# A float32 attention and two-layer MLP kernel on one core: the first weight unit in half blocks, another way to the low halves of the weights, merged steps on TensorE, another order search

## The chip, the core and the metric

The kernel runs on one core of one Trainium2 chip. The metric is the device time of one execution in microseconds (us). The engines are PE (TensorE, the matrix multiplier), DVE (VectorE), ACT (ScalarE), POOL (GpSimd) and SP (SyncE, which here only issues DMAs). PE's weight loads are listed apart from its matmuls, as PEld.

## The reference

```python
# attention: B=4, H=8, S=768, D=48
for t in range(S):
    state = alpha[:, :, t, :, None] * state + np.einsum('bhd,bhe->bhde', k[:, :, t], v[:, :, t])
    y[:, :, t] = np.einsum('bhd,bhde->bhe', q[:, :, t], state)
x = y.transpose(0, 2, 1, 3).reshape(B * S, H * D)     # 3072 tokens x 384
x = ((x @ w_a) * (x @ w_b)) @ w_out                   # first MLP, 1536 wide
h = x @ w_in                                          # second MLP, 2048 wide
g = np.maximum(h, 0.0) + alpha2 * np.minimum(h, 0.0)
out = g @ w_out2
```

The weights come as float64; everything else is float32. The output has float32 accuracy.

## The kernel before

**Three products for one.** PE's fast full-width type is fp32r, which holds fewer bits than float32. So each large operand is kept as a high part, rounded to fp32r, and a low part that holds the rest, and each product is the sum of high x high, low x high and high x low (`mm3`, lines 818, 819 and 821). A large matmul is 128 x 128 weights by 512 tokens.

**Blocks, chunks, units.** The 3072 tokens are six blocks of 512, and each block is four chunks of 128. The weights of the first MLP are six units u of 256 hidden columns; a unit has three parts, a, b (up) and o (down). One step of the first MLP is one half unit with one block: an up product `pa` (9 matmuls), an up product `pb` (9), their product on DVE (line 948), its split into `gh` (ACT, 841) and `gl` (DVE, 845), and a down product into `acc` (9). The order of these steps is the list `SEGMENTS`: block 0 with units 0 and 1, block 1 with units 0 and 1, block 0 with units 2 and 3, and so on; from block 2 on a block meets all six units. The up products keep this order. The second MLP (96 steps of 18 large matmuls) follows.

**A chunk of the attention.** The recurrence is done by chunks. On DVE: two scans and a reciprocal over alpha (523, 529, 533) and a product that scales q and k (538). On PE: the transposes of the keys (`pe_k`, 606; "keys" below), the scores (553 in block 0, 563 after), then `pe_cross` (685 and 707) and `pe_own` (685 and 692) from block 1 on. Between them DVE masks the scores (626) and adds the states (712 `mid`, 715 `kept`), ACT copies the keys out (610), and ACT and DVE split the output into the high and low part of x (770, 774). In block 1 six DMAs for each chunk (line 792) then move rows of x between partitions; the up products of that block wait for them. From block 2 on `pe_own` also computes the scores of the next chunk of the same block (`ahead`, for c < 3); the keys of each chunk are a step by themselves, and the scores of a block's first chunk too.

**A weight part.** A float64 part lies as pairs of 32-bit words. ACT takes the magnitude (368); DVE makes the sign, the float32 value, its power of two and the remainder (371, 376, 380, 385); ACT rounds to the high part (391); DVE subtracts it and adds the remainder (394, 397: the low part). For the parts a, b and o of unit 0 the last two operations are matmuls on PE (422 to 424) and a copy on ACT (427); a and b of unit 0 are also done in two halves. The parts of the second MLP take the same way later and go through HBM.

**The order.** Every operation on PE, DVE, ACT and SP is an `Op` of a `Graph` with a duration, a latency and a due time (`key`). `place` makes an order for each engine from estimated times; `search` shuffles the keys (400 tries) of operations that start early, and keeps what its cost likes; `run` emits the instructions in that order. On the chip each engine follows its own list and waits at semaphores. Where the plan has a long pause on PE before block 2, `fill` puts in small matmuls that nobody reads (`wp`, line 307), as many as `(t1 - t0) * 0.7 // 110`. The matmuls of one chunk step are a `burst` on PE.

Of the kernel before, what the change touches and what calls it, by code (L numbers as in the profile page):

```python
# [14 lines left out]
F32R = mybir.dt.float32r  # L15
I64 = mybir.dt.int64
# [6 lines left out]
P = 128  # L23
CH = 128
# [8 lines left out]
LAG = 2  # L33

# [3 lines left out]
MM = 230  # L38
# [8 lines left out]
SOON = 150000  # L47
TRIES, WORLDS = 400, 2
# [13 lines left out]
class Graph:  # L62
# [27 lines left out]
    def tables(self):  # L90
        n = len(self.ops)
        self.eng = [o.eng for o in self.ops]
        self.users = [[u.n for u in o.users] for o in self.ops]
        self.soft = [[u.n for u in o.soft] for o in self.ops]
        self.hold = [[u.n for u in o.hold] for o in self.ops]
        self.before = [[] for _ in range(n)]
        for i in range(n):
            for u in self.users[i]:
                self.before[u].append((i, True))
            for u in self.soft[i]:  # L100
                self.before[u].append((i, False))

    def place(self, keys=None, order=None, dur=None, lat=None):
# [5 lines left out]
        start, end, seq, gaps, logs = [0] * n, [None] * n, [], [], {}  # L109
        free = dict.fromkeys(eng, 0)  # L110
        able = {e: [i for i in range(n) if eng[i] == e and not need[i]] for e in free}
        burst = False

        def room(p):
            log = logs.setdefault(p, [])
# [3 lines left out]
        def when(i):  # L119
            t = room(ops[i].pool) if ops[i].pool else 0  # L120
            return None if t is None else max(ready[i], t)

        for k in range(n):
            if order is None:
                best = None
                for e, l in able.items():
                    l = [(t, i) for i in l if (t := when(i)) is not None]
                    if l:
                        t = max(free[e], min(l)[0])
                        if best is None or t < best[0]:  # L130
                            best = (t, l)
                if best is None:
                    return None
                t, l = best
                i = min((i for x, i in l if x <= t), key=lambda i: (keys[i], i))
                able[eng[i]].remove(i)
            else:
                i = order[k]
                t = when(i)
                if t is None:  # L140
                    return None
                t = max(free[eng[i]], t)
# [9 lines left out]
            if o.pool:  # L152
                logs.setdefault(o.pool, []).append(self.hold[i])
            start[i], free[e], end[i] = t, t + d, t + d + lat[i]
            seq.append(i)
            for u in self.users[i]:
                ready[u] = max(ready[u], end[i] + (HOP if eng[u] != e else 60))
            if order is None:
                for u in self.users[i] + self.soft[i]:
                    need[u] -= 1  # L160
                    if not need[u]:
                        able[eng[u]].append(u)
# [34 lines left out]
    def search(self):  # L197


        rnd, ops, n = random.Random(1), self.ops, len(self.ops)  # L200
        pe = [i for i in range(n) if self.eng[i] == "PE"]
        worlds = []
        for _ in range(WORLDS):
            worlds.append(([int(o.dur * rnd.uniform(1, 1.08)) + rnd.randrange(40) for o in ops],
                           [o.lat + (rnd.randrange(1200) if o.eng == "SP" else rnd.randrange(60)) for o in ops]))

        def cost(plan):
            if plan is None:
                return float("inf")
            plans = [plan] + [self.place(order=plan[2], dur=d, lat=l) for d, l in worlds]  # L210
            if None in plans:
                return float("inf")
            ends = [max(p[1][i] for i in pe) for p in plans]
            return ends[0] + sum(ends[1:]) / max(1, len(worlds))

        keys = [float(o.key) for o in ops]
        plan = self.place(keys)
        assert plan is not None, "the operations wait for each other"
        best = cost(plan)
        late = self.latest(*plan[:3])  # L220
        first = [i for i in range(n) if plan[0][i] < SOON]
        for k in range(TRIES):
            new = late if k == 0 else list(keys)
            if k:
                mid, width, step = rnd.uniform(0, SOON), rnd.choice((3000, 10000, 30000)), rnd.choice((2500, 8000, 24000))
                for i in first:
                    if abs(plan[0][i] - mid) < width and rnd.random() < 0.5:
                        new[i] += rnd.gauss(0, step)
            other = self.place(new)
            if other is None or max(other[1][i] for i in pe) > max(plan[1][i] for i in pe) + 1000:  # L230
                continue
            c = cost(other)
            if c <= best:
                best, keys, plan = c, new, other
        return plan
# [29 lines left out]
def body(tc, akq, v, vg, w_a, w_b, w_o1, w_in, w_o2, beta, out):  # L265
# [13 lines left out]
    with ExitStack() as ctx:  # L279
# [46 lines left out]
        flat = [(n, i, s) for s, (n, u0, u1) in enumerate(SEGMENTS) for i in range(2 * u0, 2 * u1)]  # L326
        at = [T_MOE + int(k * 27 * MM * STRETCH) for k in range(len(flat) + LAG + 1)]
        due, block_at = {}, {}
        for k, (n, i, s) in enumerate(flat):
# [8 lines left out]
        def conv(src, tag, name, key, wait, sink, early=15000, on_pe=False, halves=None):  # L338
# [11 lines left out]
            ld = G.add("SP", 2100, load, key - early, wait, 4000)  # L350
            free = cring.take()
            last, highs = [], []
            for n in range(2 if halves else 1):
# [29 lines left out]
                def rest(c2=c2, word=word):  # L383
                    o = c2()
# [3 lines left out]
                def high(n=n, c1=c1, hi=hi):  # L388
                    if n == 0:
# [10 lines left out]
                d = lambda t: t // N + 40  # L400
                m = G.add("ACT", d(910), magnitude, key, [ld, *(free if n == 0 else ())], after=last, line="c1")
                x = G.add("DVE", d(550), sign, key, [m])
                x = G.add("DVE", d(930), main, key, [x])
                x = G.add("DVE", d(550), power, key, [x])
# [736 lines left out]
```

## Time and profile before

| | |
|---|---|
| median of 3 runs | 957.52 us (957.03 to 957.98) |
| the profiled execution | 956.25 us, of which 954.5 us are the span from its first to its last instruction |
| PE busy | 943.4 us (99% of the span), 6630 matmuls |
| DVE busy | 601.9 us (63%) |
| ACT busy | 254.6 us (27%) |
| granted TensorE clock | 0.998 of 2.4 GHz over the span |
| DMA | 104.48 MB, mean 109 GB/s |

The profile shows one execution. Starts are recorded; the ends of matmuls are modelled, and neighbours overlap in the records, so a matmul's cost is read from the distance of starts and not from its duration. "Idle before" an instruction is counted from the end of the one in front of it on its engine.

### The profile page before, as it was taken

Reading aid. Unit: us, or ns where it says so; the run is one execution under the profiler, and the core shown is the slowest. Engines: PE = TensorE matmul, PEld = TensorE weight load, DVE = VectorE, ACT = ScalarE, POOL = GpSimd, SP = SyncE. Lnnn points to the kernel's source line nnn. Section 1 sums busy time; section 2 is a strip of 40 time slices with the busy share of each in tenths; the row PEclk is TensorE's granted clock in tenths of the full one; section 3 lists DMA queues with packets and bytes.
Section 4 is the critical chain, followed back from the end, with each engine's and each line's share of the span. In section 5 each row is a group of like instructions: output and inputs, shape, how many; then the busy total and the mean of one; then the engine's idle time right before and its main releaser. Section 6 shows DMA issues by size and latency. Waiting matters only on the chain.

```text
span 954.5 us, 15479 instructions
## 1 busy us (share of the span) xinstructions
PE 943.4 (99%) x6630; PEld 766.0 (80%) x6630; DVE 601.9 (63%) x883; ACT 254.6 (27%) x414; POOL 2.2 (0%) x11
## 2 busy tenths in 40 slices
PE   9989999999999999999999999999999999999998
PEld 7668888878778888888888888888888888888886
DVE  8999999576788789863232255555555545545554
ACT  2445443233333433332221211121111211111211
POOL 0000000000000000000000000000000000000000
PEclk9999999999999999999999999999999999999999
DMA  9955000244455556451164540110100200200000
GB/s 340 369 199 189 16 1 10 70 138 168 154 186 197 206 211 203 180 190 67 27 240 169 186 190 1 56 45 0 67 34 1 100 1 1 100 1 1 33 1 34
DMA packets 32228, 104.48 MB, mean 109 GB/s; under 512 B 3872, under 2 KB 5408, under 8 KB 32160
## 3 DMA queue, kind: packets, MB, share of 16 engines
q1 hardware_dynamic: 32016, 103.37, 30.7%
q8 instruction: 52, 0.85, 0.4%
q14 instruction: 16, 0.13, 0.0%
q10 hardware_dynamic: 144, 0.13, 0.0%
HBM read 74.78 MB, written 26.74 MB: 106 GB/s over the span
## 4 chain that ended last, share of the span: by engine, by line
PE 95%; DVE 4%; issue 0%; ACT 0%; POOL 0%; ACTq 0%; DVEq 0%; POOLq 0%
PE acc L821 12%; PE acc L818 12%; PE acc L819 12%; PE pi L818 7%; PE pi L819 7%; PE pi L821 7%; PE pa L818 5%; PE pb L818 5%; PE pa L819 5%; PE pa L821 5%; PE pb L819 5%; PE pb L821 5%; PE both L685 2%; PE both L563 1%; PE both L692 1%; PE wp L307 1%
## 5 line engine op out<-in xcount | busy, mean ns | idle before, releaser
L841 ACT CAST gh<-ng 128x512 fp32r<-128x512 f32 x96 | 59.6, 621 | 318.9 <-DVE ng L1054 256.4
L1050 DVE TENSOR_SCALAR ng<-pi,betaT 128x512 f32<-128x512 f32 x96 | 72.1, 751 | 106.1 <-PE pi L821 105.7
L845 DVE TENSOR_TENSOR gl<-ng,gh 128x512 fp32r<-128x512 f32 x96 | 66.3, 690 | 78.3 <-ACT gh L841 78.3
L821 PE MATMUL acc<-gl,v 128*128 128x512 f32 x288 | 113.5, 394 | 0.0
L819 PE MATMUL acc<-gh,v 128*128 128x512 f32 x288 | 112.9, 392 | 0.0
L818 PE MATMUL pi<-x,v 128*128 128x512 f32 x288 | 112.8, 392 | 0.0
L819 PE MATMUL pi<-x,v 128*128 128x512 f32 x288 | 112.7, 391 | 0.0
L818 PE MATMUL acc<-gh,v 128*128 128x512 f32 x288 | 111.8, 388 | 0.0
L948 DVE TENSOR_TENSOR a_sb<-a_sb,pb 128x512 f32<-128x512 f32 x72 | 49.4, 685 | 93.6 <-PE pb L821 93.1
L818 PE MATMUL pa<-x,wa 128*128 128x512 f32 x216 | 87.3, 404 | 0.0
L818 PE MATMUL pb<-x,wb 128*128 128x512 f32 x216 | 86.4, 400 | 0.0
L818 PE MATMUL acc<-gh,wo 128*128 128x512 f32 x216 | 86.1, 398 | 0.0
L819 PE MATMUL pa<-x,wa 128*128 128x512 f32 x216 | 85.1, 394 | 0.0
L821 PE MATMUL acc<-gl,wo 128*128 128x512 f32 x216 | 85.0, 394 | 0.0
L819 PE MATMUL pb<-x,wb 128*128 128x512 f32 x216 | 84.6, 391 | 0.0
L819 PE MATMUL acc<-gh,wo 128*128 128x512 f32 x216 | 84.5, 391 | 0.0
L821 PE MATMUL pi<-x,v 128*128 128x512 f32 x288 | 81.5, 391 | 0.0
L945 ACT COPY a_sb<-pa 128x512 f32<-128x512 f32 x72 | 42.2, 586 | 135.0 <-PE pa L821 134.9
L841 ACT CAST gh<-a_sb 128x512 fp32r<-128x512 f32 x72 | 44.7, 621 | 117.8 <-DVE a_sb L948 102.3
L1054 DVE SCALAR_TENSOR_TENSOR ng<-pi,ng 128x512 f32<-128x512 f32 x96 | 66.3, 691 | 3.0
L819 PEld LDWEIGHTS acc<-gh,v 128*128 128x128 f32 x288 | 54.0, 188 | 12.6
L818 PEld LDWEIGHTS pi<-x,v 128*128 128x128 f32 x288 | 54.1, 188 | 12.2 <-DVE ng L1054 0.4
(118 smaller groups left out, 1410.5 us busy)
## 6 DMA issues: line engine op xcount, KB each, us to landing
kq<-in_akq SPq DMA_DIRECT2D x24, 512.0 KB, 4.5
w2d<-ws SPq DMA_DIRECT2D x16, 768.0 KB, 3.5
v<-w2d SPq DMA_DIRECT2D x16, 768.0 KB, 5.4
x2d<-x SPq DMA_DIRECT2D x18, 512.0 KB, 3.4
x<-x2d SPq DMA_DIRECT2D x6, 1536.0 KB, 6.9
ra<-in_akq SPq DMA_DIRECT2D x24, 258.5 KB, 4.1
v<-in_v SPq DMA_DIRECT2D x24, 256.0 KB, 5.0
rs<-in_w_in SPq DMA_DIRECT2D x8, 768.0 KB, 4.6
```

The costliest lines, as they stand in the source:

```text
L307: nc.tensor.matmul(wp, warm[:, 0:P], warm, start=True, stop=True)
L563: nc.tensor.matmul(a[hs, i, j, :], kT()[ps, j, hs], qT()[ps, j, hs], start=True, stop=True, skip_group_check=True)
L685: nc.tensor.matmul(y_of(k, half(p), part_of(h)), s["v"][part_of(h), 2 * j + i, :], s["As"][part_of(h), i, j, :], start=first, stop=False, ...
L818: nc.tensor.matmul(o, lh, rh, start=first and n == 0, stop=False)
L819: nc.tensor.matmul(o, ll, rh, start=False, stop=False)
L821: nc.tensor.matmul(o, lh, rl, start=False, stop=last and n == len(pairs) - 1)
L841: nc.scalar.copy(gq[idx][0], src())
L845: nc.vector.tensor_tensor(out=gl, in0=src(), in1=gh.bitcast(F32), op=ALU.subtract)
L945: nc.scalar.copy(b["a"], ba["t"])
L948: nc.vector.tensor_tensor(out=b["a"], in0=b["a"], in1=bb["t"], op=ALU.mult)
L1050: nc.vector.tensor_scalar(out=b["n"], in0=bh["t"], scalar1=0.0, scalar2=betaT[:, i : i + 1], op0=ALU.min, op1=ALU.mult)
L1054: nc.vector.scalar_tensor_tensor(out=b["n"], in0=bh["t"], scalar=0.0, in1=b["n"], op0=ALU.max, op1=ALU.add)
```

## The change

Six edits:

1. **Half blocks.** `SPLIT` names unit 0 with block 0. Its two steps of 512 tokens become four of 256: tokens 0 to 255 with both half units, then 256 to 511. The first two need x of chunks 0 and 1 alone.
2. **Low parts.** For all parts but those of unit 0: the low word and the low bits of the high word are put together into one signed 32-bit number (`top`, in place in the raw words; `below`), ACT makes the high part with a scale (`rounded`), and the low part is that number times the power of two of the value (`exponent`, `low`). On DVE: 371, 376, `top`, `below`, `exponent`, `low` instead of 371, 376, 380, 385, 394, 397.
3. **Low parts on PE.** For a and b of unit 0 the remainder is written as fp32r, and the third matmul is fp32r instead of float32.
4. **Merged steps.** From block 1 on keys and scores are one step (`both_of`: scores, then transposes). From block 2 on `pe_own` of each chunk is followed by scores and keys of the next chunk (`ahead["both"]`), across the end of a block too. That step now waits also for the next chunk's scaled q and k and for the bank of the transposes.
5. **Search.** Another walk: it starts from the latest start times, accepts some worse plans, 500 tries, only operations that start in the first 120 us; two other random "worlds" with less scatter; `place` keeps heaps.
6. **Estimates.** The first load is put at 1000 + 2400 ns instead of 3200 + 1500, a load of weights at 2000 + 3500 instead of 2100 + 4000, a large matmul at 229 ns instead of 230, and others by 10 to 30 ns.

```diff
+SPLIT = ((0, 0),)
-MM = 230
+MM = 229
-SOON = 150000
-TRIES, WORLDS = 400, 2
+SOON = 120000
+SEED, TRIES, WORLDS = 6, 500, 2
...
+        plan = self.place([o.key for o in ops])
+        keys = self.latest(*plan[:3])
+        plan = self.place(keys) or plan
+        best = now = (cost(plan), keys, plan)
+        rnd = random.Random(SEED)
         for k in range(TRIES):
+            new, begin = list(now[1]), now[2][0]
+            width, share = rnd.choice(((1500, 0.6), (1500, 0.6), (5000, 0.3), (15000, 0.12), (50000, 0.04)))
+            mid, step = rnd.uniform(0, SOON), rnd.choice((2000, 7000, 25000))
+            for i in range(n):
+                if begin[i] < SOON and abs(begin[i] - mid) < width and rnd.random() < share:
+                    new[i] += rnd.gauss(0, step)
+            plan = self.place(new)
+            if plan is None or last(plan) > last(now[2]) + 1000:
                 continue
+            c = cost(plan)
+            if c <= now[0] or rnd.random() < math.exp((now[0] - c) / (100 * (1 - k / TRIES) + 1)):
+                now = c, new, plan
+                best = min(best, now, key=lambda x: x[0])
...
-        flat = [(n, i, s) for s, (n, u0, u1) in enumerate(SEGMENTS) for i in range(2 * u0, 2 * u1)]
+        whole, parts = slice(0, MB), (slice(0, MB // 2), slice(MB // 2, MB))
+        flat = [(n, 2 * u + o, s, t) for s, (n, u0, u1) in enumerate(SEGMENTS) for u in range(u0, u1)
+                for t in (parts if (n, u) in SPLIT else (whole,)) for o in range(2)]
+        span = lambda t: MM if t == whole else MM // 2 + 10
+        size = lambda t, ns: ns if t == whole else ns // 2 + 80
...
-                def sub(c1=c1, hi=hi):
-                    nc.vector.tensor_tensor(out=c1(), in0=c1(), in1=hi().bitcast(F32), op=ALU.subtract)
+                def top(word=word):
+                    nc.vector.tensor_scalar(out=word(1, U32), in0=word(1, U32), scalar1=23, scalar2=None,
+                                            op0=ALU.logical_shift_left)
+                def below(c2=c2, word=word):
+                    nc.vector.scalar_tensor_tensor(out=c2().bitcast(U32), in0=word(0, U32), scalar=9,
+                                                   in1=word(1, U32), op0=ALU.logical_shift_right,
+                                                   op1=ALU.bitwise_or)
+                def rounded(n=n, c1=c1, hi=hi):
+                    b["r"] = wpool.tile([P, 2 * UC], F32R, name=f"w{name}", tag=tag)
+                    nc.scalar.mul(hi(), c1(), 1.0 + 2.0**-22)
+                def exponent(c1=c1):
+                    x = c1().bitcast(U32)
+                    nc.vector.tensor_scalar(out=x, in0=x, scalar1=0xFF800000, scalar2=None, op0=ALU.bitwise_and)
                 def low(c1=c1, c2=c2, lo=lo):
-                    nc.vector.tensor_tensor(out=lo(), in0=c1(), in1=c2(), op=ALU.add)
+                    nc.vector.scalar_tensor_tensor(out=lo(), in0=c2().bitcast(I32), scalar=2.0**-43,
+                                                   in1=c1(), op0=ALU.mult, op1=ALU.mult)
                     sink(b["r"])
...
-                        nc.tensor.matmul(o, ident, cut(c2()), start=False, stop=True)
+                        nc.tensor.matmul(o, *((plus, cut(lo())) if halves else (ident, cut(c2()))),
+                                         start=False, stop=True)
...
-            la = A("SP", 3200 if g == 0 else 720, load_a, rwait, 14000, 1500 if g == 0 else 3000, line="ra")
+            la = A("SP", 1000 if g == 0 else 720, load_a, rwait, 14000, 2400 if g == 0 else 3000, line="ra")
...
+            def keys():
+                s["kps"] = (s["kbank"] if start else att)("kps")
+                for j in range(NJ):
+                    nc.tensor.transpose(s["kps"][:, j, :], kT()[:, j, :], ident)
+            def both_of():
+                scores()
+                keys()
...
-            ahead = st[g + 1] if n > 1 and c < BC - 1 else None
+            ahead = st[g + 1] if n > 1 and g + 1 < NG else None
...
+            elif "front" in s:
+                x = pa = s["front"]
+                khold = s["khold"]
+            else:
+                x = pa = A("PE", 1150, s["both"], [k1, *aring.take(), *afree, *yfree])
+                khold = aring.last()
...
                     if ahead:
-                        ahead["scores"]()
+                        ahead["both"]()
...
+                if ahead:
+                    py = A("PE", 1900, pe_own, [z1, z2, ahead["k1"], *aring.take()])
+                    ahead.update(front=py, khold=aring.last())
+                    ahead["lhold"].append(py)
-                py = A("PE", 1460 if ahead else 900, pe_own, [z1, *([z2, ahead["k1"]] if ahead else ())])
...
+            xs = xdone[n] if t == whole else xdone[n][t.start // CH : t.stop // CH]
+            pa, ma, ba = up(at[k], [done["a", u][o], *xs], x, ("a", u), o, [up_before], t)
+            pb, mb, bb = up(at[k] + 9 * span(t), [done["b", u][o], *xs], x, ("b", u), o, [pa], t)
```

## Rows read from the trace of the kernel before

**Rows 1.** Stretches: length, then busy us (instructions) by engine, PE clock, DMA share, GB/s.

```profile
9.60:67.40 57.80, 51.72 (x801) 39.80 (x800) 55.92 (x93) 23.58 (x48) 0.00 (x0) 0.99 0.88 328
66.30:69.70 3.40, 3.34 (x38) 2.78 (x39) 3.40 (x6) 1.86 (x4) 0.00 (x0) 0.51 0.43 154
110.00:550.00 440.00, 440.00 (x3755) 356.83 (x3754) 289.21 (x425) 141.29 (x224) 0.00 (x0) 1.00 0.42 143
```

**Rows 2.** Timeline of PE, 66 to 69 us: start, us, instruction, idle before it.

```profile
66.36 1.14 PE L563 MATMUL both<-kq 48*64 48x64 f32 x32 [1.77 <-DVE x L774]
67.42 0.79 PE L818 MATMUL pa<-x,wa 128*128 128x512 f32 x1
```

**Rows 3.** Timeline of DVE, 10 to 76 us.

```profile
10.82 0.69 DVE L622 TENSOR_TENSOR As<-A,mask 128x512 f32<-128x512 f32 x1 [0.50 <-PE A L553]
...
64.75 0.95 DVE L397 TENSOR_TENSOR wa<-c,c 128x768 fp32r<-128x768 f32 x1
...
69.15 0.55 DVE L371 TENSOR_SCALAR c<-ro 128x768 uint32<-128x768 uint32 x1
...
75.42 0.69 DVE L774 TENSOR_TENSOR x<-both,x 128x512 fp32r<-128x512 f32 x1
```

**Rows 4.** Timeline of SP's DMA queue, 75 to 92 us.

```profile
76.14 4.68 SPq L792 DMA_DIRECT2D x<-x  x6
```

**Rows 5.** Timeline of PE, 84 to 89 us.

```profile
86.45 0.85 PE L821 MATMUL pa<-x,wa 128*128 128x512 f32 x3
...
88.51 0.85 PE L821 MATMUL pb<-x,wb 128*128 128x512 f32 x3
```

**Rows 6.** Timeline of PE, 163 to 166 us, around own with scores.

```profile
163.73 0.40 PE L821 MATMUL acc<-gl,wo 128*128 128x512 f32 x1
...
165.70 0.39 PE L819 MATMUL pa<-x,wa 128*128 128x512 f32 x1
```

**Rows 7.** Timeline of PE, 195 to 199 us, around own, scores and keys.

```profile
195.66 0.85 PE L821 MATMUL pa<-x,wa 128*128 128x512 f32 x3
...
198.47 0.39 PE L819 MATMUL pb<-x,wb 128*128 128x512 f32 x1
```

**Rows 8.** Timeline of PE, 236 to 239 us, around keys alone.

```profile
236.74 0.85 PE L821 MATMUL pb<-x,wb 128*128 128x512 f32 x3
...
238.10 0.40 PE L819 MATMUL acc<-gh,wo 128*128 128x512 f32 x1
```

**Rows 9.** Timeline of PE, around own alone, then around keys with scores.

```profile
285.27 0.85 PE L821 MATMUL pa<-x,wa 128*128 128x512 f32 x3
...
287.23 0.40 PE L819 MATMUL pb<-x,wb 128*128 128x512 f32 x1
...
323.40 0.85 PE L821 MATMUL pb<-x,wb 128*128 128x512 f32 x3
...
325.58 0.40 PE L819 MATMUL pa<-x,wa 128*128 128x512 f32 x1
```

**Rows 10.** Groups by line and shape: count, busy us, mean ns, idle us before.

```profile
L371 DVE TENSOR_SCALAR c<-ro 128x768 uint32<-128x768 uint32 x6 | 3.3, 551 | 0.0
L397 DVE TENSOR_TENSOR wa<-c,c 128x768 fp32r<-128x768 f32 x5 | 4.8, 950 | 0.0
L424 PE MATMUL cl<-c,plus 128*128 128x384 f32 x12 | 4.8, 485 | 0.0
L819 PEld LDWEIGHTS pa<-x,wa 128*128 128x128 f32 x216 | 41.0, 190 | 8.3
L948 DVE TENSOR_TENSOR a_sb<-a_sb,pb 128x512 f32<-128x512 f32 x72 | 49.4, 685 | 93.6 <-PE pb L821 93.1
L774 DVE TENSOR_TENSOR x<-both,x 128x256 fp32r<-128x256 f32 x4 | 1.6, 408 | 0.0
```

**Rows 11.** DMA issues: count, KB each, median us to landing.

```profile
x<-x SPq DMA_DIRECT2D x24, 64.0 KB, 3.2
ra<-in_w_a SPq DMA_DIRECT2D x6, 768.0 KB, 7.5
```

More of the change, by code (lines that the diff above doesn't have):

```diff
@@ L108, in place @@
         need, ready = [len(b) for b in self.before], [0] * n
-        start, end, seq, gaps, logs = [0] * n, [None] * n, [], [], {}
+        start, end, seq, gaps, logs = [0] * n, [None] * n, [], [], {p: [] for p in self.pools}
         free = dict.fromkeys(eng, 0)
-        able = {e: [i for i in range(n) if eng[i] == e and not need[i]] for e in free}
+        later, able = {e: [] for e in free}, {e: [] for e in free}
+        pooled = []
         burst = False
         def room(p):
-            log = logs.setdefault(p, [])
+            log = logs[p]
@@ L136, in place @@
-                able[eng[i]].remove(i)
+                t = None
+                for x in free:
+                    l, a, f = later[x], able[x], free[x]
+                    while l and l[0][0] <= f:
+                        i = heapq.heappop(l)[1]
+                        heapq.heappush(a, (keys[i], i))
+                    at = f if a else l[0][0] if l else None
+                    if x == "PE":
+                        pools = [(max(f, ready[i], b), keys[i], i) for i in pooled
+                                 if (b := room(ops[i].pool)) is not None]
+                        at = min([at] * (at is not None) + [q[0] for q in pools], default=None)
+                    if at is not None and (t is None or at < t):
+                        t, e = at, x
@@ L207, in cost @@
         def cost(plan):
[L208 to L217, printed above, removed]
+            plans = [self.place(order=plan[2], dur=d, lat=l) for d, l in worlds]
@@ L218, in search @@
+            return float("inf") if None in plans else (last(plan) + sum(map(last, plans)) / len(plans)) / 2
+        plan = self.place([o.key for o in ops])
         assert plan is not None, "the operations wait for each other"
-        best = cost(plan)
-        late = self.latest(*plan[:3])
-        first = [i for i in range(n) if plan[0][i] < SOON]
+        keys = self.latest(*plan[:3])
+        plan = self.place(keys) or plan
+        best = now = (cost(plan), keys, plan)
+        rnd = random.Random(SEED)
@@ L222, in search @@
         for k in range(TRIES):
[L223 to L230, printed above, removed]
-                continue
@@ L232, in search @@
[L232 to L235, printed above, removed]
+            new, begin = list(now[1]), now[2][0]
+            width, share = rnd.choice(((1500, 0.6), (1500, 0.6), (5000, 0.3), (15000, 0.12), (50000, 0.04)))
+            mid, step = rnd.uniform(0, SOON), rnd.choice((2000, 7000, 25000))
+            for i in range(n):
+                if begin[i] < SOON and abs(begin[i] - mid) < width and rnd.random() < share:
+                    new[i] += rnd.gauss(0, step)
@@ L413, in conv @@
                     continue
+                x = G.add("DVE", d(550), power, key, [x])
+                x = G.add("DVE", d(950), rest, key, [x])
+                x = G.add("ACT", d(840), high, key, [x], after=highs)
+                highs = [x]
                 ev = None
@@ L845, in lo, with down @@
                 nc.vector.tensor_tensor(out=gl, in0=src(), in1=gh.bitcast(F32), op=ALU.subtract)
-            h = G.add("ACT", 620, hi, key, [*deps, *gring.take()], line="gh")
-            return G.add("DVE", 700, lo, key, [h])
-        def down(idx, key, deps, hold, acc, w, o, first, last):
+            h = G.add("ACT", size(t, 620), hi, key, [*deps, *gring.take()], line="gh")
+            return G.add("DVE", size(t, 680), lo, key, [h])
+        def down(idx, key, deps, hold, acc, w, o, first, last, t=whole):
             def f():
```

206 lines of the change are left out of this document (110 added, 96 removed).

## Prediction

> **What bounds the kernel now.** I read the table of stretches first. From 110 to 550 us PE is busy in all 440.0 us while DVE works 289 of them; from 9.6 to 67.4 us PE is busy in 51.7 of 57.8 us and DVE in 55.9 [rows 1]. So there are two stages. In the late one the time is the sum of PE's steps: nine large matmuls lie between the two starts of [rows 5], 88.51 - 86.45 = 2.06 us, 0.229 us each, and nothing but shorter or fewer steps on PE can help. In the head DVE is the bound: PE's idle time there is 57.80 - 51.72 = 6.1 us, and some of its busy time is fill.
>
> Next the timelines, to find which DVE instruction ends PE's waiting for good. The longest wait ends at 66.36, behind a DVE split [rows 2]; the first up product of unit 1 starts at 67.42 [rows 2], after the low part of that weight (64.75 + 0.95 = 65.70, [rows 3]). The waiting has a second price: from 66.3 to 69.7 us the granted clock is 0.51, the 1.2 GHz level [rows 1]. At full clock this work of 3.4 us takes about half, so 1.6 us went there.
>
> There is a second date close behind. Block 1 starts when x of chunk 7 has been moved: its low part at 75.42 [rows 3], six DMAs issued from 76.14 for 4.68 us [rows 4], the last landing some 3.2 us later [rows 11], at 84.0. Block 1's first up product starts six matmuls before 86.45, at 85.08 [rows 5]. So the head can move by 1.1 us before chunk 7 too must come earlier.
>
> **Merged steps.** The price of a chunk step on PE is the distance from the last large matmul before it to the second one behind it, less the 2 x 0.229 us that these two would take (a row "x3" starts two matmuls earlier). Own with scores: 165.70 - 163.73 - 0.46 = 1.51 [rows 6]. Keys alone: 238.10 - 236.74 - 0.92 = 0.44 [rows 8]. Own, scores and keys in one, which the old order once happened to make: 198.47 - 195.66 - 0.92 = 1.89 [rows 7]. So a chunk that goes from 1.95 to 1.89 saves 0.06: 12 chunks in blocks 2 to 5, one of which had it, 0.7 us. Where a block begins the gain is larger: own alone 287.23 - 285.27 - 0.92 = 1.04, keys with scores 325.58 - 323.40 - 0.92 = 1.26 [rows 9], together 2.30 against 1.89, 0.41 each for blocks 3, 4 and 5: 1.2 us. Block 1's four steps lie in the head, and I count nothing for them. Sum: **-1.9 us** in a stage where PE never idles. What the merge costs is a longer list of things to wait for: own of a block's last chunk now also waits for the next block's scaled keys, and PE's whole queue stands behind it. The cover is DVE's slack, 151 of 440 us [rows 1]; without it one late chunk costs what DVE needs for it, a few us.
>
> **Low parts.** Removed per part are 0.55 (380) + 0.95 (385) + 0.95 (394) + 0.95 (397) = 3.40 us of DVE; added are `top`, `below`, `exponent`, `low`. The two with two tensors are like line 397, 0.95; the two with one tensor and a constant are like line 371, which reads every second word in 0.55 [rows 10]. That is 3.00, so -0.40 a part. `top` also writes every second word, which no row shows: it is between 0.55 and 0.95, and I take 0.55 for its likeness to 371; the other end makes the edit worth nothing. Before the date of 67.42 parts a and b of unit 1 count: **-0.8 us**. Later parts lie where PE is the bound, and count nothing.
>
> The Trainium skill (VectorE: DVE Perf Modes, "Mode 2×_2P — use both read ports for one tensor") lets an operation with a single tensor in SBUF run at two float32 results a cycle and names no condition on the step; by it `top` is 0.55 and the sum stays; by the slow row it would lose 0.8.
>
> **Half blocks.** On DVE the product and the split of a step are 685 ns each, and an operation on 256 columns 408 [rows 10]: 2 x 408 - 685 = 0.13, for two operations of two steps **+0.5 us**. On PE 108 matmuls of 256 columns replace 54 of 512. Free would be 0.1145 each; the other end is the record of a weight load, 0.190 [rows 10], so 0 to +8.2 us. I take +1, nearer to the free end, since at 0.229 the loads hide with nearly as much work behind them; it falls where PE has 6.1 us of idle time, so nothing of it reaches the end. In return block 0 can meet its first weights with two chunks done instead of four.
>
> A rule speaks against this edit: the Trainium skill (TensorE: Matmul & The Clock Gate, "LDWEIGHTS (loading the stationary operand)") puts a load at its columns over 1.2 GHz, 107 ns for 128 of them, however few columns then stream; by it the half matmul is just covered, by the record it would be bound by its load.
>
> **Third matmul of a and b.** Four float32 products leave, at most 4.8 / 6 = 0.8 us each [rows 10], so 0 to -3.2 us of PE work before 54 us. PE waits for DVE later in the head, so this only lengthens that wait: 0.
>
> **Estimates and fill.** The first score matmuls come late enough that DVE waits 0.50 for them at 10.82 [rows 3]; with the first load put at 3.4 us instead of 4.7 the plan's first pause, and with it the fill, is about 1.3 us shorter. **-0.5 us** of DVE time. It cancels the +0.5 of the half blocks.
>
> **Order.** How much can another order give? DVE's list before chunk 7's split at 75.42 holds work that nothing needs so soon: four operations of o of unit 1 from 69.15 [rows 3] (0.55 + 0.95 + 0.55 + 0.95 = 3.0) and three of unit 2's a (0.55 + 0.95 + 0.55 = 2.05), 5 us. Between 0 and -5 I take **-1.0**, as the chains from PE to ACT to DVE must fit between. With it and the -0.8 the wait before 66.36 (1.77 and another before it) breaks up enough that the clock stays up: **-1.6**, or 0 if it does not.
>
> **Sum.** -1.9 - 0.8 + 0.5 - 0.5 - 1.0 - 1.6 = -5.3 us. The profiled execution took 956.25 (span 954.5 and 1.75 around it), and would take 950.9; the median of the runs is 957.52, so 952.2 is what I predict for the median. A measurement can tell about 0.2%, 1.9 us: faster is below 955.6, slower above 959.4.
>
> **Rivals.**
> 1. *The second date holds.* If chunk 7 does not move, the head gives only the 1.1 us between 84.0 and 85.08: 957.5 - 1.9 - 1.1 = 954.5. For it: its chain goes through PE, ACT and six DMAs, which no edit shortens. Against it: the 5 us of work that can be put behind it.
> 2. *The order finds most of the slack.* -1.9 - 0.8 - 1.6 - 5 = 948.2. Against it: DVE would have to do everything in the best order with no gap.
> 3. *The head gives nothing*, since `top` is slow, the half blocks' DVE work eats the rest, and the clock falls in some other wait: 957.5 - 1.9 = 955.6, or up to 957.5 if the merged steps wait as much as they save. That is the case where the change does not do what it says.
> 4. *Slower: loads land late under a tighter plan.* DVE follows its list in order. The new plan reckons 5.5 us for a load of weights (before 6.1); the rows say 7.5 [rows 11], with the DMA engines at 0.88 over the head [rows 1]. Each load that is 2.0 us late for its first operation stops the scans and splits behind it by as much, and a clock drop adds 1.6. It turns slower from 7.2 us of such stalls on; three late loads and one drop, 7.6, give 957.5 - 5.3 + 7.6 = 959.8. Against it: the old plan was wrong by 1.4 too, and DVE was still busy in 55.9 of 57.8 us [rows 1].
>
> **How the numbers follow.** Forecast 0.55 (its own range 949.5 to 953.7), second date 0.18, most of the slack 0.10, nothing from the head 0.10, slower 0.07. The range that leaves out 2 in 10 reaches from the order's bound, 948.5, into the third rival, 956.0. Faster: 0.55 + 0.18 + 0.10 = 0.83; the third rival is the same, 0.10; slower 0.07.
>
> **What would show it.** In the new profile: `pe_own` steps of 1.89 us from block 2 on, no separate transposes after it, and PE still busy in all of 110 to 540 us; `top` at 0.55; starts of the half matmuls some 0.12 us apart; the first up product of unit 1 and that of block 1 both some 3 us before 67.42 and 85.08; no stretch at 0.51 of the clock after the first fill. I am wrong if block 1's first up product is not earlier, if DVE shows waits for DMA in the head, or if PE waits in the late stage.

## The result, and the profile after

The changed kernel takes 949.23 us (median of 4 runs, 948.92 to 949.48) against 957.39 (957.03 to 957.98) for the kernel before: 0.9914 of it [0.9897, 0.9931], 8.2 us faster. The profiled execution took 949.33 with a span of 947.6; 6.9 us of span are gone against the profiled 954.5 of before. The other 1.2 or so lie in the kernel before, whose runs lie above its profiled one (956.28 to 957.62 over thirteen later runs, mean granted clock 0.996 to 0.998); with the change the four runs show a clock of 1.000. The clock alone doesn't explain the 1.2: of those thirteen runs the ten at 0.998 spread from 956.28 to 957.57.

**Stretches after**, in the columns of [rows 1]: first the three stretches shown there, then 9.6 us to chunk 7's split and to block 1's first up product, and three slices of 25 us from 75 us on.

```profile
9.60:67.40 57.80, 55.48 (x906) 45.06 (x904) 57.52 (x103) 26.39 (x55) 0.00 (x0) 1.00 0.90 339
66.30:69.70 3.40, 3.40 (x108) 2.94 (x107) 3.40 (x8) 1.18 (x2) 0.00 (x0) 1.00 0.25 68
110.00:550.00 440.00, 440.00 (x3733) 358.29 (x3733) 275.56 (x422) 140.38 (x220) 0.00 (x0) 1.00 0.43 148
...
9.60:71.44 61.84, 59.52 (x971) 48.53 (x970) 61.56 (x110) 28.33 (x58) 0.00 (x0) 1.00 0.87 327
9.60:78.85 69.25, 66.93 (x1007) 54.78 (x1006) 68.97 (x122) 32.41 (x64) 0.00 (x0) 1.00 0.85 318
...
75.00:100.00 25.00, 25.00 (x111) 20.51 (x110) 25.00 (x39) 12.67 (x18) 0.00 (x0) 1.00 0.25 88
100.00:125.00 25.00, 25.00 (x185) 20.24 (x184) 25.00 (x41) 12.59 (x19) 0.00 (x0) 1.00 0.04 11
125.00:150.00 25.00, 25.00 (x187) 20.50 (x186) 24.99 (x38) 11.76 (x17) 0.00 (x0) 1.00 0.15 43
```

**The same two dates and slices of the kernel before.**

```profile
9.60:75.42 65.82, 59.74 (x918) 46.02 (x918) 63.80 (x106) 26.35 (x53) 0.00 (x0) 0.97 0.83 307
9.60:85.08 75.48, 69.40 (x961) 53.91 (x960) 73.45 (x122) 32.26 (x61) 0.00 (x0) 0.98 0.81 302
...
75.00:100.00 25.00, 25.00 (x111) 20.51 (x110) 24.13 (x36) 13.94 (x21) 0.00 (x0) 1.00 0.39 146
100.00:125.00 25.00, 25.00 (x111) 20.52 (x110) 24.66 (x36) 10.78 (x18) 0.00 (x0) 1.00 0.04 12
125.00:150.00 25.00, 25.00 (x188) 20.29 (x187) 23.36 (x36) 10.54 (x16) 0.00 (x0) 1.00 0.01 1
```

Up to chunk 7's split, DVE's idle time fell from 65.82 - 63.80 = 2.02 us to 0.28, and its busy time from 63.80 to 61.56. Up to block 1, PE's idle time fell from 6.08 to 2.32 us, and its busy time by 2.5 us, in which the stretch at 0.51 of the clock [rows 1] lies. In the slices from 75 to 150 us DVE has no gap left, and PE has none either.

**The waits of PE after**, engine, line and what it waited for: us in total, times, longest. All three rows of the answer:

```profile
PE both L624 <- DVE x L843: 1.7, 3, 1.0
PE wp L338 <- POOL ones L340: 1.4, 1, 1.4
PE kps L630 <- issue: 0.4, 1, 0.4
```

The 1.77 behind the split [rows 2] is now at most 1.0.

**Timeline of PE after**: the half matmuls, the first up product of unit 1 (60.63), PE's last wait before block 1 (63.22), block 1's first up product (78.85), and one merged step.

```profile
28.85 0.28 PE L888 MATMUL pa<-x,wa 128*128 128x256 f32 x1
28.97 0.28 PE L887 MATMUL pa<-x,wa 128*128 128x256 f32 x1
...
29.44 0.51 PE L890 MATMUL pa<-x,wa 128*128 128x256 f32 x3
...
60.63 0.51 PE L887 MATMUL pa<-x,wa 128*128 128x512 f32 x1
...
63.22 0.69 PE L624 MATMUL both<-kq 48*64 48x64 f32 x32 [0.23 <-DVE x L843]
...
78.85 0.39 PE L887 MATMUL pa<-x,wa 128*128 128x512 f32 x1
...
189.35 0.85 PE L890 MATMUL pa<-x,wa 128*128 128x512 f32 x3
190.13 0.46 PE L749 MATMUL both<-As,v 64*64 64x64 f32 x16
...
190.86 0.65 PE L624 MATMUL both<-kq 48*64 48x64 f32 x32
191.44 0.66 PE L630 MATMUL kps<-plus,kq 128*128 128x128 f32 x4
...
192.16 0.39 PE L888 MATMUL pb<-x,wb 128*128 128x512 f32 x1
```

Unit 1 starts 6.8 us earlier than the 67.42 of [rows 2], block 1 6.2 us earlier than the 85.08 worked out from [rows 5]. The merged step costs 192.16 - 189.35 - 0.92 = 1.89 us, as [rows 7].

**From PE's last wait to block 1**, before and then after, in the columns of [rows 1]. PE has no gap in either.

```profile
66.36:85.08 18.72, 18.72 (x192) 15.05 (x192) 18.57 (x31) 9.42 (x15) 0.00 (x0) 0.91 0.62 228
...
63.22:78.85 15.63, 15.63 (x195) 13.13 (x196) 15.63 (x28) 7.91 (x12) 0.00 (x0) 1.00 0.67 236
```

**Timeline of DVE after**, where [rows 3] stood: the first scores, the low part of unit 1's first weight, chunk 7's split.

```profile
11.31 0.69 DVE L691 TENSOR_TENSOR As<-A,mask 128x512 f32<-128x512 f32 x1 [0.28 <-PE A L614]
...
59.42 0.95 DVE L452 SCALAR_TENSOR_TENSOR wa<-c,c 128x768 fp32r<-128x768 int32 x1
...
71.44 0.68 DVE L843 TENSOR_TENSOR x<-both,x 128x512 fp32r<-128x512 f32 x1
```

**SP's DMA queue after**, beside [rows 4]:

```profile
72.15 3.77 SPq L861 DMA_DIRECT2D x<-x  x6
```

**The last of the six DMAs in the kernel before**, and the times from an issue to its landing of all six:

```profile
80.22 0.59 SPq L792 DMA_DIRECT2D x<-x  x1
...
DMA to landing us min/median/max: 1.8/3.9/5.1
```

**Groups by line and shape after**, beside [rows 10]: `top`, and a product of half width.

```profile
L433 DVE TENSOR_SCALAR ra<-ra 128x768 uint32<-128x768 uint32 x5 | 2.8, 557 | 0.0
L1018 DVE TENSOR_TENSOR a_sb<-a_sb,pb 128x256 f32<-128x256 f32 x4 | 1.6, 405 | 0.0
```

**Where the 6.9 us of span come from.** Block 1 starts 6.23 us earlier. Behind that point the chunk steps cost 47.49 us in sum instead of 49.33, each priced as in the prediction: -1.84. That makes -8.07, and 1.24 are given back in the second MLP, as follows; 0.1 us stays unassigned.

**Timeline of PE after, at the end of a block of the second MLP.**

```profile
621.10 0.39 PE L887 MATMUL pi<-x,v 128*128 128x512 f32 x1
...
622.47 0.85 PE L890 MATMUL pi<-x,v 128*128 128x512 f32 x3
623.30 0.51 PE L887 MATMUL pi<-x,v 128*128 128x512 f32 x1
623.65 0.40 PE L888 MATMUL pi<-x,v 128*128 128x512 f32 x1
```

**Timeline of DVE after, at the same place.**

```profile
621.30 0.75 DVE L1120 TENSOR_SCALAR ng<-pi,betaT 128x512 f32<-128x512 f32 x1 [0.58 <-PE pi L890]
621.97 0.68 DVE L915 TENSOR_TENSOR gl<-ng,gh 128x512 fp32r<-128x512 f32 x1
622.57 0.68 DVE L1124 SCALAR_TENSOR_TENSOR ng<-pi,ng 128x512 f32<-128x512 f32 x1
```

The table of PE's waits has no row for this, and PE counts as busy throughout, since the modelled end of one matmul covers the gap. It shows in the distance of starts, and in the table of waits of the weight loads (PEld), here after and then before: six waits instead of one.

```profile
PEld pi L887 <- DVE ng L1124: 2.5, 6, 0.4
...
PEld pi L818 <- DVE ng L1054: 0.4, 1, 0.4
```

In starts it reads like this. The group of nine that starts at 621.10 has its ninth matmul at 622.47 + 2 x 0.229 = 622.93. From there to the second matmul of the next group, 623.65, two steps of 0.229 would take 0.46, and took 0.72: 0.26 lost. That next group starts 0.05 us after DVE's line 1124 has read the bank `pi` (622.57 + 0.68 = 623.25). DVE is not short of time there: it stood idle for 0.58 us just before 621.30. But between its two readings of that bank (lines 1120 and 1124) it makes the split of the product before (line 915), so the bank comes free 623.25 - 621.30 = 1.95 us after the first reading began. With two banks PE needs it again after one up product in the other bank, 2.06 us, and the passing from PE to DVE and back doesn't fit into the rest. Five such ends (622.9, 689.1, 755.3, 821.5, 887.7) are new, 1.24 us in all; the one at 556.8 has its like in the kernel before, at 565.

### The profile page after: what moved, and what is told of

It is laid out like the page before. It is cut to its first block, busy times and chain, and to the rows that moved or that the text cites. A ratio compares the mean times of both kernels' runs of the same rounds, so it can differ in the third digit from the quotient of the medians.

```text
span 947.6 us, 15534 instructions
## 1 busy us (share of the span) xinstructions
PE 940.3 (99%) x6671; PEld 766.1 (81%) x6671; DVE 587.2 (62%) x887; ACT 256.1 (27%) x418; POOL 2.2 (0%) x11
## 4 chain that ended last, share of the span: by engine, by line
PE 94%; DVE 5%; issue 1%; POOL 0%; ACT 0%; DVEq 0%; ACTq 0%; POOLq 0%
PE acc L887 12%; PE acc L888 12%; PE acc L890 12%; PE pi L887 7%; PE pi L888 7%; PE pi L890 7%; PE pb L887 5%; PE pa L887 5%; PE pb L890 5%; PE pb L888 5%; PE pa L890 5%; PE pa L888 5%; PE both L749 1%; PE kps L630 1%; PE wp L338 1%; PE both L624 1%
## 5 line engine op out<-in xcount | busy, mean ns | idle before, releaser
L1018 DVE TENSOR_TENSOR a_sb<-a_sb,pb 128x512 f32<-128x512 f32 (+1 forms) x74 | 49.5, 669 | 100.6 <-PE pb L890 99.6
L887 PE MATMUL pa<-x,wa 128*128 128x512 f32 (+1 forms) x222 | 87.1, 394 | 0.0
L887 PE MATMUL acc<-gh,wo 128*128 128x512 f32 (+1 forms) x222 | 86.6, 390 | 0.0
L887 PE MATMUL pb<-x,wb 128*128 128x512 f32 (+1 forms) x222 | 86.5, 391 | 0.0
L890 PE MATMUL acc<-gl,wo 128*128 128x512 f32 (+1 forms) x222 | 85.9, 387 | 0.0
L888 PE MATMUL acc<-gh,wo 128*128 128x512 f32 (+1 forms) x222 | 85.3, 384 | 0.0
L888 PE MATMUL pa<-x,wa 128*128 128x512 f32 (+1 forms) x222 | 85.2, 385 | 0.0
L888 PE MATMUL pb<-x,wb 128*128 128x512 f32 (+1 forms) x222 | 85.2, 385 | 0.0
L911 ACT CAST gh<-a_sb 128x512 fp32r<-128x512 f32 (+1 forms) x74 | 45.2, 610 | 140.2 <-DVE a_sb L1018 129.1
L1015 ACT COPY a_sb<-pa 128x512 f32<-128x512 f32 (+1 forms) x74 | 42.6, 576 | 118.7 <-PE pa L890 118.4
L1124 DVE SCALAR_TENSOR_TENSOR ng<-pi,ng 128x512 f32<-128x512 f32 x96 | 66.3, 691 | 3.0
```

The costliest lines, as they stand in the source:

```text
L887: nc.tensor.matmul(o, lh, rh, start=first and n == 0, stop=False)
L888: nc.tensor.matmul(o, ll, rh, start=False, stop=False)
L890: nc.tensor.matmul(o, lh, rl, start=False, stop=last and n == len(pairs) - 1)
L911: nc.scalar.copy(gq[idx][0], src())
L1015: nc.scalar.copy(b["a"], ba["t"])
L1018: nc.vector.tensor_tensor(out=b["a"], in0=b["a"], in1=bb["t"], op=ALU.mult)
```

## The experiments

The theory I began with was the prediction's: DVE's list in the head is the bound, some edits shorten it, and a better order takes more. Its rivals were that the new search alone does it, and that the edits alone do. In each group all kernels were timed against the kernel before on one chip; it took 957.33, 956.89 and 957.37 us (medians) in the three groups, so raw medians of different groups can be compared to about 0.5 us. "After" is the changed kernel, 949.23.

### First group: search, seed and one estimate

**The new edits with the old search.**

```diff
-SOON = 120000
-SEED, TRIES, WORLDS = 6, 500, 2
+SOON = 150000
+TRIES, WORLDS = 400, 2
```

The body of `search` is that of the kernel before, too.

> The changed kernel with the old search (400 tries from the first plan, the old random worlds, 150 us). In the changed kernel the first up product of block 1 came 6.2 us earlier (85.08 to 78.85) and the merged steps took 1.8 us off the late stage. Theory 'order' (the new search found most of the 6.2): the head falls back by 3 us or more, 952 to 956. Theory 'edits' (half blocks, low parts and the shorter third matmul give any search this room): within 1.5 us of the changed kernel, 949 to 951.

951.26 us, 0.9940 [0.9925, 0.9955]. Block 1's first up product starts at 80.44. So 6.1 of the 8.2 us are there with the old search; the new one adds 2.0 with seed 6, and 0.4 with seed 1 (950.89, below).

**The old edits with the new search.**

```diff
-SOON = 150000
-TRIES, WORLDS = 400, 2
+SOON = 120000
+SEED, TRIES, WORLDS = 6, 500, 2
```

The lines are against the kernel before, which gets `place` and `search` of the changed one and nothing else.

> The kernel before with nothing but the new search. Theory 'order': 4 us or more of the 6.2 come with the search alone, 951.5 to 953.5. Theory 'edits': the old graph has no room, 955.5 to 957.5.

957.38 us, 1.0002 [0.9993, 1.0011]. Block 1 starts at 85.72 and unit 1 at 67.60, both a little later than before, and the clock still falls (its stretch, in the columns of [rows 1]):

```profile
66.30:69.70 3.40, 2.81 (x37) 2.31 (x38) 3.40 (x6) 1.87 (x3) 0.00 (x0) 0.66 0.79 307
```

That rules out the search, with this seed, as a cause by itself: on the old edits it found nothing.

**Another seed.**

```diff
-SEED, TRIES, WORLDS = 6, 500, 2
+SEED, TRIES, WORLDS = 1, 500, 2
```

> The changed kernel with seed 1 in place of 6: how far the order alone moves the time. Theory 'order': 1 to 3 us off, 949 to 952. Theory 'edits': the same within 0.7 us.

950.89 us, 0.9936 [0.9921, 0.9951]; block 1 at 78.43, 0.4 us earlier than with seed 6, and yet 1.7 us slower at the end. The date misleads here: nine large matmuls of a down product, 9 x 0.229 = 2.06 us, stand behind block 1's first up product with this seed and in front of it with seed 6 (9 and 18 matmuls of 512 tokens write `acc` before that date). Counted alike, block 1 would come at 80.5, 1.6 later, which is nearly all of the 1.7. Two seeds differ by 1.7 us, so a single search is no ruler for an edit of this size.

**The estimate of the second MLP's stores.** The five new stalls at the ends of blocks are also there with the old search and with seed 1 (six waits of PEld for line 1124 each), and not in the old edits with the new search (one), so the new edits or estimates bring them. The plan puts the eviction of an output tile late because it reckons its store at 1400 + 2000 ns. This run changes that one line.

```diff
-                    ring.use(G.add("ACT" if h else "SP", 1400, store, key - URGENT, [x], 2000))
+                    ring.use(G.add("ACT" if h else "SP", 700, store, key - URGENT, [x], 1300))
```

> The changed kernel with one estimate changed, that of the output stores of the second MLP (700 + 1300 ns in place of 1400 + 2000). Up to 550 us all orders stay as they were; at the five block borders of the second MLP three up products stand in a row in place of four. In the changed kernel each of these borders shows a pair of starts on PE 0.25 us late. Theory: DVE needs 0.75 + 0.69 + 0.69 = 2.13 us for each up product in a row and PE 2.06, so the fourth waits for its bank; with three in a row 1.2 us come back, 948.0. Rival: the waiting moves to the down products behind them, 949.2.

947.78 us, 0.9902 [0.9886, 0.9919]: 1.45 faster than after, at the same start of block 1 (78.75), with the same order up to 550 us. PE at the same end of a block:

```profile
622.39 0.85 PE L890 MATMUL pi<-x,v 128*128 128x512 f32 x3
623.08 0.39 PE L887 MATMUL acc<-gh,v 128*128 128x512 f32 x1
623.31 0.39 PE L888 MATMUL acc<-gh,v 128*128 128x512 f32 x1
```

A down product now stands where a further up product stood, there are three up products in a row instead of four, and the distance is 623.31 - 622.39 - 0.92 = 0.00. Five stalls are gone, and the one at 556.7 is left: PEld has one such wait. The stalls and their price are shown. Which of the other changed estimates tipped the order was not tried.

### Second group: one edit undone, the search run anew

**No half blocks.**

```diff
-SPLIT = ((0, 0),)
+SPLIT = ()
```

> The changed kernel without the half blocks (unit 0 meets block 0 in steps of 512 tokens again), searched anew. The first two runs showed that the search gives nothing to the old graph and that the new graph gives 6 us with the old search; two seeds differ by 1.7 us, so smaller differences may be the order's. Theory 'half blocks': PE has about 12 us of fill and waiting before 67 us, and half steps put block 0's first products there, so this costs 3 us or more: 952 or above. Rival 'DVE': DVE is the bound, the half blocks only add 0.5 us to it, so without them 948.5 to 949.5.

952.10 us, 0.9949 [0.9935, 0.9964]; block 1 at 81.22, 2.4 us later than after. PE spends more of the head in fill; the fill alone, without half blocks and then after (busy us and count, PE clock, DMA share, GB/s):

```profile
9.60:81.22 71.62, 10.31 (x79) 1.00 0.86 319
...
9.60:78.85 69.25, 7.07 (x51) 1.00 0.85 318
```

**The old low parts.** `sub` and the old sum in place of `exponent` and `low`, and `power` and `rest` in place of `top` and `below`.

```diff
-                    x = G.add("DVE", 550, top, key, [x])
-                    x = G.add("DVE", 950, below, key, [x])
-                    x = G.add("ACT", 840, rounded, key, [x])
-                    x = G.add("DVE", 550, exponent, key, [x])
-                    x = G.add("DVE", 950, low, key, [x])
+                    x = G.add("DVE", 550, power, key, [x])
+                    x = G.add("DVE", 950, rest, key, [x])
+                    x = G.add("ACT", 840, high, key, [x])
+                    x = G.add("DVE", 950, sub, key, [x])
+                    x = G.add("DVE", 950, low_sum, key, [x])
```

> The changed kernel with the old low parts (0.95 + 0.95 after the rounding, 3.40 us of DVE a part in place of 3.00) for all parts but unit 0's, searched anew. Theory 'DVE': what lies before block 1's first product counts (a, b and most of o of unit 1), and DVE has no gap there: +1.2, or 950.4, a little more if what DVE does for later units also pushes. Rival 'half blocks': PE's free time takes it, 949.2 to 949.7.

951.53 us, 0.9943 [0.9927, 0.9960]; block 1 at 80.89, 2.0 us later than after. From there to the end of the span it takes 868.7 us, as after, so with an order of its own this edit costs its time in the head.

**Both undone**: no half blocks and the old low parts in one kernel.

> Both undone: old low parts and no half blocks; the merged steps, the shorter third matmul, the new search and the new estimates stay. If the two edits add up, the sum of what they cost alone. If both together are the head's gain of 6 us, 955 to 955.5 (the merged steps' 1.8 us are left). If 953 or less, the shorter third matmul, block 1's merged steps or the estimates hold a good part of the head's gain.

954.18 us, 0.9973 [0.9961, 0.9985]; block 1 at 83.88. With old low parts the half blocks are worth 954.18 - 951.53 = 2.65. What is left against the kernel before, 2.7 us, is the merged steps, the third matmul, the estimates and the search together.

**The third matmul of a and b of unit 0 in float32**, as before the change.

```diff
-                    o = lo() if halves else c2()
+                    o = c2()
...
-                        nc.tensor.matmul(o, *((plus, cut(lo())) if halves else (ident, cut(c2()))),
+                        nc.tensor.matmul(o, ident, cut(c2()),
                                          start=False, stop=True)
...
-                    y = G.add("PE", 1080 if halves else 1560, add, key, [x], pool=mpool)
+                    y = G.add("PE", 1560, add, key, [x], pool=mpool)
```

> The changed kernel with the third matmul of a and b of unit 0 in float32 as before: four products that take about 0.5 us more each on PE, before 45 us. My prediction: this only changes how long PE waits, 949.2 (to 950.0). Rival: PE is as tight as DVE in the head now, and the 2 us come back in full: 951.2.

952.42 us, 0.9955 [0.9940, 0.9969]; block 1 at 83.08. Taken at its word, this would make the third matmul worth 3.2 us, the whole of its upper bound. But its changed estimate also set off another search. The third group separates the two.

### Third group: the order held, and more tries

**The old low parts in the order of after.** As the old low parts above, but `sub` is planned at 550 ns, so that the plan sees the same durations and every engine's list stays as it is. The lines are against the kernel with the old low parts.

```diff
-                    x = G.add("DVE", 950, sub, key, [x])
+                    x = G.add("DVE", 550, sub, key, [x])
```

> The changed kernel with the old operations of the low parts at the same places of the same order (the planner is told the new durations, so every list stays as it is): one of the five operations behind the value takes 0.95 in place of 0.55 on DVE, 0.4 us more a part, and nothing else differs. Undoing the low parts with a new search cost 2.3 us. Theory 'DVE one to one': a and b of unit 1 lie before the last product of unit 1 and o before block 1's first, three parts, and DVE has no gap there: +0.8 to +1.2, 950.0 to 950.4; the rest of the 2.3 was the order. Rival: a late part stalls a list that fits the new durations, +2.3 or more, 951.5 or above.

953.62 us, 0.9963 [0.9948, 0.9977]: 4.4 us slower than after. A stretch of its trace, in the columns of [rows 1]:

```profile
110.00:160.00 50.00, 47.41 (x325) 38.18 (x325) 49.98 (x75) 21.94 (x33) 0.00 (x0) 1.00 0.08 22
```

Its table of PE's waits, the row for DVE's products:

```profile
PE pb L894 <- DVE a_sb L1025: 2.6, 2, 1.4
```

Its timeline of PE, the two places:

```profile
111.23 0.50 PE L894 MATMUL pb<-x,wb 128*128 128x512 f32 x1 [1.20 <-DVE a_sb L1025]
...
140.78 0.50 PE L894 MATMUL pb<-x,wb 128*128 128x512 f32 x1 [1.39 <-DVE a_sb L1025]
```

Block 1 starts at 79.72, only 0.9 us later than after. The rest comes behind it: PE waits 2.6 us for DVE's products, at 111 and at 141 us, where after has no wait; by the distance of starts these two places cost 3.1. Chunk 7's split is 0.95 late (72.39 for 71.44), the first operation of a weight part at 131.14 is 4.6 late (135.70), a split at 154.09 is 5.75 late (159.84). DVE loses some 0.4 us with every part and never gets it back before 155 us, as it has no gap there.

**The third matmul in float32 in the order of after.** As in the second group, with the estimate left at 1080; every engine's list stays as it is.

> The changed kernel with the third matmul of a and b of unit 0 in float32 at the same places of the same order: 0.48 us more on PE four times before 46 us. With a new search this cost 3.2 us. Theory 'only PE waits longer' (my prediction): what PE has then it waits for DVE, 949.2 to 949.7, and the 3.2 were the order. Rival 'PE is as tight': +1.5 to +1.9, 950.7 to 951.1. Third: the copies on ACT and the releases behind these products delay DVE too, +3, 952 or above.

949.38 us, 0.9917 [0.9903, 0.9932]; block 1 at 78.98. The edit is worth 0.15 us, nothing that can be told from zero. The same edit with its search run anew cost 3.2: so 3 us is what a new search alone can do to a variant. The differences of the second group are uncertain by as much.

**No half blocks with seed 1**: `SPLIT = ()` and seed 1 in one kernel.

> Without half blocks, seed 1 in place of 6; the pair to the changed kernel with seed 1 (950.9). With seed 6 the half blocks were worth 2.9 us. Theory 'half blocks': 2 to 4 us again, 953 to 955. Rival: the 2.9 were the order's, 950 to 952.

951.47 us, 0.9944 [0.9927, 0.9960]; block 1 at 80.68. Against half blocks with the same seed (950.89) the edit is worth 0.6 us; with seed 6 it was 2.9. So the pair that was to confirm the 2.9 did not.

**The store estimate and 2000 tries.** The store line of the first group, and:

```diff
-SEED, TRIES, WORLDS = 6, 500, 2
+SEED, TRIES, WORLDS = 6, 2000, 2
```

> The kernel with the other estimate for the output stores (947.8) and 2000 tries in place of 500. Theory 'the head is at DVE's bound': block 1's first product at 78.75 needs what DVE has done by then, and no order gives more than 1 us: 947 to 948. Rival 'there is still slack in the order': 946.5 or below.

947.71 us, 0.9901 [0.9886, 0.9916], the same as with 500 tries (947.78). This version and that one beat both kernels. Four times the tries of this search find nothing more. DVE is busy in 68.97 of the 69.25 us up to block 1 in the kernel after, but some of that is work that block 1 doesn't need so soon (`wa` of unit 2 from 69.03 on), so it is not shown that no other order gives more.

## Why the prediction was right, and where its steps were not

I predicted 952.2 us, faster with 0.83. The direction and the mechanism held: the head, bound by DVE, gives most of it, and the merged steps the rest. The kernel is 3.0 us faster than my figure: inside the range of 948.5 to 956.0, but 0.3 us past the end of the forecast's own (949.5 to 953.7), and near the second rival's time. The head gave 6.2 where its terms came to 3.4, about twice, and its terms one by one were mostly not right, as follows; that the total stays inside the range all the same is in part luck.

**Merged steps: right.** -1.84 where I had -1.9, at 1.89 to 1.90 us a step. PE doesn't idle between 110 and 550 us, so the longer list of things to wait for did no harm.

**Clock: right.** The stretch from 66.3 to 69.7 us runs at 1.00 instead of 0.51 [rows 1]. Behind the first fill no wait of PE is longer than 1.0 us. The kernel before has this loss in its other runs too, with a mean clock of 0.996 to 0.998; whether that is the 1.2 us by which its median lies above its profiled run is not shown. The price was not measured by a run, but the trace bears it out: before, the scores and the nine up matmuls behind them take 70.71 - 66.36 = 4.35 us, and after, such scores take 63.85 - 63.22 = 0.63 and such nine matmuls 71.64 - 69.44 = 2.20, 1.5 us less.

**Low parts: the mechanism was right, the size was not.** `top` takes 552 to 557 ns, the fast end of my bound. The Trainium skill's rule for a single tensor (VectorE: DVE Perf Modes, "Mode 2×_2P — use both read ports for one tensor") would make `top` as fast as line 371, 0.55, and the trace agrees, with every second word written. A part saves the 0.4 us that I reckoned. What failed is the sentence "Later parts lie where PE is the bound, and count nothing". With the order held, the old low parts cost 4.4 us instead of 0.8, and 3.5 of them appear behind block 1's start. I had read DVE's slack over 110 to 550 us as one number, 151 of 440 [rows 1]. The slices show that almost none of it lies before 125 us: in the kernel before DVE is already busy for 24.13 and 24.66 of 25 us there. A share of a long stretch says nothing of its beginning. The 4.4 hold for an order that was made for the shorter operations. With the search run anew the old low parts cost 2.3, and none of that lies behind block 1's start (868.7 us from there to the end in both kernels).

**Half blocks: probably a gain, and not settled.** I had +0.5 on DVE, cancelled by the earlier scores. Half operations take 405 to 412 ns on DVE as reckoned, and half matmuls start 0.118 us apart ((29.44 - 28.85) / 5), close to the free end of 0.1145. The record of a weight load, 0.190 [rows 10], is not the limit. The Trainium skill's 107 ns for 128 columns (TensorE: Matmul & The Clock Gate, "LDWEIGHTS (loading the stationary operand)") allows it, and the trace agrees. The edit was worth 2.9, 2.65 and 0.6 us in three pairs of runs, each with its search run anew. All three have one sign, but the scatter of the search is as large: that it gains is likely, and neither that nor how much is shown. My sum had it as a cost; what I left out is that it gives both engines work when little else is ready. The first half product starts at 28.63; without half blocks PE spends 10.31 us up to block 1 in fill where after has 7.07, and DVE idles 0.8 us (busy in 70.82 of 71.62) where after has 0.28. That fits, but each of the two kernels has an order of its own, so it is not shown to be the reason; with both edits undone DVE idles only 0.1 us up to block 1, so in that pair its gaps are not.

**Third matmul: right,** 0.15 us with the order held.

**Estimates and fill: wrong, and small.** I expected the first scores earlier. DVE's first score operation comes at 11.31, later than the 10.82 of [rows 3], though DVE waits 0.28 us for it instead of 0.50. Nor was the first fill shorter: it ends at 10.11 after and at 9.63 before. The estimates did not give the 0.5, and they or the edits around them brought the stalls of the second MLP, 1.24 us, which I had not looked for: I took it that nothing in that stage is touched.

**Order.** I gave the order -1.0 by itself. By itself the new search gives 0.0 on the old edits, and on the new ones 2.0 with seed 6 and 0.4 with seed 1. All of this is within its scatter, so a worth of the new search is not shown.

**The rivals.** The first, that the second date holds, falls: chunk 7's split came 3.98 us earlier. Of that, 1.74 us are closed gaps of DVE and 2.24 less work in front of it (the two stretches up to that date). The date itself was misread. [rows 11] counts from each issue's own start, and the last of the six DMAs starts at 80.22 and lands 1.8 us later, at about 82 and not at 84.0, so the head had some 3 us of room before chunk 7 and not 1.1. After, the last one lands at 77.1, still 1.7 us before block 1's first up product. PE doesn't wait for it in either kernel: what sets block 1's start is the end of PE's last wait for DVE, and the work that PE has then still to do. That wait ends 66.36 - 63.22 = 3.14 us earlier, and the work behind it takes 15.63 us instead of 18.72, 3.09 less, some 1.5 of it the clock: 6.23 in all. The second rival's time, 948.2, was nearly reached, but the order alone did not do it. The third falls with the 6.2 us. The fourth falls too: a load of a part of w_a still takes 7.4 us to land, and yet DVE waits for no weight. Its only wait for a DMA up to 100 us is the first load's 3.7, as before.

**Open** are whether the half blocks gain and how much, what the new search is worth, which estimate or edit brought the stalls (the six waits are also there without half blocks, with the old low parts, with both undone and with the third matmul in float32, which points to the merged steps or the estimates), and how the 2.7 us that remain without low parts and half blocks are shared. Merging across the end of a block was not tried apart.

## What to carry to other kernels

Read the busy share of the engine that is not the bound in slices of 25 us, not over the whole stage: work that it is spared can count for as long as it has no gap. Where a search sets the order, undo an edit with the planned durations kept, or the scatter of the search (3 us here) passes for the worth of the edit. After any change of estimates, look at the distance of starts, and at the waits of the weight loads, at places that the change doesn't touch, since a stall of 0.25 us between matmuls shows in no row of PE's own waits.

## What was not expected of the hardware

Nothing against the prediction, which looked for 0.12. Still worth keeping: matmuls of 256 columns, each with a weight load in front of it, start 0.118 us apart, a little over half of the 0.229 of 512 columns, although the record of a load in the same kernels is 0.188 to 0.190 us long. In these kernels the record of a weight load is thus no bound on the rate of matmuls.
